# Tile tokens interleaved by four over the 32x32 blocks, one rearranging store per tile, q and k loaded per tile

## The chip, the cores and the metric

The kernel runs on one core of a Trainium2 chip. The metric is the device time of one execution in microseconds (us). Three runs of the kernel before took 1748.88 to 1751.74 us, with a median of 1751.24 us.

## What is computed

Three layers run one after the other on 8 batches of 576 tokens with a model width of 512, all in float32.

```python
# attention inside chunks of 64 tokens, 8 heads of 64
scores = scale * (q_c @ k_c.T); attn = softmax(scores); x = attn @ v_c     # (B, S, 512)
# first layer: layer norm, then a feed-forward of width 2048, with a residual
xn = (x - mean(x)) / sqrt(var(x) + 1e-6) * g_ln
x = x + relu(xn @ w_ch1) @ w_ch2
# second layer: low-rank mixing over the sequence, then another feed-forward
u = x + (x.T @ U @ V).T
out = u + relu(u @ w2_ch1) @ w2_ch2
```

The weights and U, V come as 8-byte floats; the kernel turns each weight into a high and a low float32 part and multiplies in three passes (high by high, high by low, low by high).

## The kernel before, in words

The 4608 tokens are 36 tiles of 128 tokens, three tiles to a block, so 12 blocks (0 to 11). A tile holds two chunks of 64. One program order is written out by hand in steps: in step `g` TensorE does the first product of one (block, f) pair (`g1`, 12 matmuls into the bank `psh`) and the second product of the pair two steps earlier (`g2`, 9 matmuls into `acc`). A block takes 16 steps. Between them the plan puts the attention and the normalisation of the tiles of the next block, and the turning of the second layer's weights (`pre_*`). Each engine runs its share of this one order, and waits where an operand is not there.

For blocks 3 to 11 (27 tiles) a tile passes these stages, in steps counted from a tile's start `s`. With `g` the first step of the block before its own, `s` is `g-3`, `g+1`, `g+5` for the three tiles from block 6 on, a little later for blocks 3 to 5:

- `load_qk` (SP queue, line 335): q and k of one block, features on the partitions, in pieces of 32 floats (128 bytes).
- `st_A` (VectorE, lines 379 and 380): two 32x32-block transposes, into `qt` and `kt_pl`.
- `st_Bd` (TensorE, tile `psm<-kt_pl,qt`, one step after `st_A` for the first tile of a block): scores, then maximum, subtraction and exponential (ScalarE, line 487).
- `st_Cd`: `spread` stores the exponentials in a DRAM scratch `sp` (ScalarE's queue, line 604), so that `gather` (line 609) can load the tile with its 32-blocks exchanged.
- `st_T` (VectorE, line 503): a transpose of what was gathered. `st_D`: the product with v (TensorE, `psm<-v_pl,kt_pl`; v comes by `load_v`, line 362).
- `st_N`, `st_S`, `st_E`: the normalised tile `xn` makes the same trip, `spread`, `gather`, and a transpose on VectorE (line 614), then the split in high and low parts (ScalarE line 616, GpSimd line 617). They are the right-hand side of `g1` of the tile's block.

A 32x32 transpose turns blocks in place on the partitions, so `spread` and `gather` exchange the blocks between partitions. Before, token `t` of a tile has block `a = t // 32` and place `j = t % 32`; a store that takes `a` off the partitions needs a DMA of its own for each of the four `a`.

Two more things of the program matter. The ReLU of `g1` (ScalarE line 677, high part, then VectorE line 678, low part) must be done before `g1` uses the same bank again, two steps later; it stands in order on ScalarE and VectorE behind what the plan puts there, the DMA issues of ScalarE's queue among them. And every DMA takes the next of eight completion semaphores in program order, whichever queue issues it; a DMA waits until the one eight places before it has landed. `load_qk` for a whole block waits until `st_A` of the last tile of the block before has read the tile `q6` or `k6`. The raw weight words (tile `raw`, lines 179 and 182) are loaded on SP's queue too, and are read first by ScalarE (`pre_a`, line 190).

Of the kernel before, what the change touches and what calls it, by code (L numbers as in the profile page):

```python
# [8 lines left out]
F32 = mybir.dt.float32  # L9
# [9 lines left out]
def fused_kernel(ctx, tc, q, k, v, g_ln, w1_a, w2_a, U, V, w1_b, w2_b, out):  # L19
    nc = tc.nc  # L20
# [4 lines left out]
    P = 128  # L25
    CH = 64
    NCB = S // CH
    NT = B * S // P
    TPB = 3
    BT = TPB * P  # L30
    NB = NT // TPB
    NF = DFF // P
    SB = (7, 7, 8, 7, 7)
    PRE_G, PRE_N = 168, (11, 22)
    PRE_GAPS = (4, 1, 1, 1, 1, 1, 4, 1)
    PRE_SKIP, PRE_CAP = (15, 0), {"POOL": 1}
    NPR = NF // 2
    KT = DM // P
# [10 lines left out]
    qkp = ctx.enter_context(tc.tile_pool(name="qkp", bufs=1))  # L49
# [15 lines left out]
    def f32(a):  # L65
        return a.bitcast(F32)
# [244 lines left out]
    def chunk_runs(c0, n):  # L311
        done = 0
        while done < n:
            b, s = divmod(c0 + done, NCB)
            m = min(n - done, NCB - s)
            yield done, m, b, s * CH
            done += m

    qk = {}

    def load_qk(j, part, parts_):
        todo = []
        for nm in ("q6", "k6"):
            if nm not in qk:
                qk[nm] = qkp.tile([P, 4, 4 * TPB, 32], F32, tag=nm, name=nm)
        for off, n, b, s0 in chunk_runs(2 * TPB * j, 2 * TPB):
            for nm, src in (("q6", q), ("k6", k)):
                for g in range(4):
                    for pr in range(4):
                        todo.append((  # L330
                            qk[nm][32 * g:32 * g + 32, pr, 2 * off:2 * (off + n), :],
                            src[b, 2 * pr + g // 2, s0:s0 + n * CH, (g % 2) * 32:(g % 2) * 32 + 32].rearrange("(a j) i -> j a i", j=32),
                        ))
        for o, i_ in todo[part * len(todo) // parts_:(part + 1) * len(todo) // parts_]:
            nc.sync.dma_start(out=o, in_=i_)  # L335

    E0 = 2 * TPB
    pl = {}
# [33 lines left out]
    def st_A(i):  # L376
        j, t = divmod(i, TPB)
        qt = t1.tile([P, 4, P], F32, tag="qt", name="qt")
        nc.vector.transpose(out=qt.rearrange("p h (a j) -> p h a j", a=4), in_=qk["q6"][:, :, 4 * t:4 * t + 4, :])
        nc.vector.transpose(out=pl["k"][:, 0].rearrange("p h (a j) -> p h a j", a=4), in_=qk["k6"][:, :, 4 * t:4 * t + 4, :])  # L380
        state["qt", i] = qt


# [106 lines left out]
    def st_Cd(i):  # L490
        e = state.pop(("e", i))
        spread(2 * NT + i, e)
        s2 = st.tile([P, 2, 2, 4], F32, tag="s2", name="s2")
        nc.vector.tensor_reduce(out=s2.rearrange("p h k r -> p (h k r)"), in_=e.rearrange("p (g i) -> p g i", i=32), axis=AX.X, op=ALU.add)
        sm = st.tile([P, H, 1], F32, tag="sm", name="sm")
        nc.vector.scalar_tensor_tensor(out=sm.rearrange("p (r h) o -> p h (r o)", h=2), in0=s2[:, :, 0, :], scalar=1e-9, in1=s2[:, :, 1, :], op0=ALU.add, op1=ALU.add)
        nc.vector.reciprocal(out=sm, in_=sm)
        state["s", i] = sm

    def st_T(i):  # L500
        w = state.pop(("w", 2 * NT + i))
        pt = pl["k"][:, 1]
        nc.vector.transpose(out=pt.rearrange("p r (a j) -> p a r j", a=4), in_=w.rearrange("p a (r i) -> p a r i", r=4))
        state["p", i] = (pt, state.pop(("s", i)))

    xt = {}
# [62 lines left out]
    def tiles_of(j):  # L569
        return [j * TPB + t for t in range(TPB)]  # L570

    def xt_tile(j, t):
        if t == 0:
            n = KT * P * len(tiles_of(j))
            o = (2 * n + 3 * BT) * (j % 2)
            xt[j] = tuple(act[:, o + m * n:o + (m + 1) * n].rearrange("p (k c) -> p k c", k=KT) for m in range(2))
        return (a[:, :, t * P:(t + 1) * P] for a in xt[j])
# [22 lines left out]

    def spread(key, src):
        d = dr.tile([4, 32, 4, P], F32, tag=f"sp{key}", name=f"sp{key}")
        for a in range(4):
            nc.scalar.dma_start(out=d[:, :, a, :].rearrange("g j c -> j g c"), in_=src[32 * a:32 * a + 32, :].rearrange("j (g c) -> j g c", g=4))
        state["sp", key] = d

    def gather(key):
# [3 lines left out]

    def split(j, t, w, tag):
        x = t1.tile([P, KT, P], F32, tag=tag, name="wT")
        nc.vector.transpose(out=x.rearrange("p k (a j) -> p a k j", a=4), in_=w.rearrange("p a (k i) -> p a k i", k=KT))
        hi, lo = xt_tile(j, t)
        nc.scalar.copy(out=hi, in_=x)  # L616
        nc.gpsimd.tensor_tensor(out=lo, in0=x, in1=f32(hi), op=ALU.subtract)  # L617

    def st_S(i):
        spread(i, state.pop(("n", i)))  # L620

    def st_E(i):
        split(i // TPB, i % TPB, state.pop(("w", i)), "xn")
# [88 lines left out]
    def stages(s):  # L712
        return (0, 1, 2, 3, 4, 6, 5) if s + 1 < len(SB) else range(7)

# [6 lines left out]
    NWR, NHR = 15, 8  # L721
    row0 = [sum(SB[:s]) * P for s in range(len(SB))]
    ncol = [SB[s] * P // 2 for s in range(len(SB))]
    made = {}
# [86 lines left out]
    def batches(s):  # L811
        c = 0
        while c < SB[s] * P:
            b, v0 = divmod(row0[s] + c, S)
            n = min(S - v0, SB[s] * P - c)
            yield b, c, v0, n
# [143 lines left out]
    def z_tile(s, t):  # L960
        if (s, t) not in zout:
            if s == len(SB) - 1 and t < 4:
                zout[s, t] = made["u", (s + 1) % 2][t][0]
# [169 lines left out]
    with tc.manual_schedule():  # L1133
# [12 lines left out]
        def at(g, fn, *a):  # L1146
            plan.setdefault(g, []).append((fn, a))
# [9 lines left out]
        for n in range(2, NB):  # L1157
            g = NF * (n - 1)
            ends = []
            for t, i in enumerate(tiles_of(n)):  # L1160
                if n == 2:
                    s = (10, 15, 24)[t]
                    at(s - 6, load_qk_nat, i)
                    at(s, st_A_pe, i)
                    at(s + 1, st_B, i)
                    at(s + 2, st_C, i)
                    at(s + 3, st_D, i)
                    at(s + 3, load_v, i + 1)
                    if t == 0:
                        at(5, kv_tiles, i)  # L1170
                        at(6, load_v, i)
                    ends += [(pos[0, NF - 1] - 1 + t, st_N, i), (pos[0, NF - 1] + t, st_E_pe, i)]
                else:
                    s = g + {3: (2, 5, 8), 4: (-1, 2, 5), 5: (-2, 1, 5)}.get(n, (-3, 1, 5))[t]
                    at(s - (1 if n < 5 or t == 0 else 2), st_A, i)
                    at(s, st_Bd, i)
                    at(s + 1, st_Cd, i)
                    at(s + 2, gather, 2 * NT + i)
                    at(s + 3, st_T, i)
                    at(s + 5, st_D, i)  # L1180
                    if i + 1 < NT:
                        at(s + 5, load_v, i + 1)
                    s += 4 if n == 3 else 6
                    at(s + (n == 3), st_N, i)
                    at(s + 1, st_S, i)
                    at(s + 2, gather, i)
                    at(s + 3, st_E, i)
            for x in sorted(ends, key=lambda x: (x[0], x[1] is st_N)):
                at(*x)
            if 2 <= n < NB - 1:  # L1190
                runs = len(list(chunk_runs(2 * TPB * (n + 1), 2 * TPB)))
                first, last = {2: (13, 16), 3: (8, 12), 4: (4, 9)}.get(n, (3, 9) if runs == 1 else (0, 9))
                parts_ = last + 1 - first
                for part in range(parts_):
                    at(g + first + part, load_qk, n + 1, part, parts_)
        for n in range(NB):
            g = pos[n, NF - 1] + 1
            at(g + LAG + 2, store, n)
            g = max(g, pos[1, NF - 1] + 1)
            both = any((n * TPB + t) % 9 == 4 for t in range(TPB))  # L1200
            early_z = []
            for t in range(TPB):
                i = n * TPB + t
                r = i % 9
# [59 lines left out]
        x = PRE_G  # L1264
# [88 lines left out]
        for g in range(len(seq) + LAG):  # L1353
# [19 lines left out]
            j, f = seq[g - LAG] if LAG <= g < len(seq) + LAG else (0, 0)  # L1373
# [42 lines left out]
```

## Time and profile before

| | |
|---|---|
| median of three runs | 1751.24 us (1748.88 to 1751.74) |
| the profiled execution | 1754.48 us, its span 1752.7 us |
| TensorE busy | 1660.1 us, 95% of the span |
| VectorE, ScalarE, GpSimd busy | 1186.0, 599.2, 300.3 us |
| mean granted clock of TensorE | 0.977 |
| DMA packets under 512 bytes | 197857 of 388847 |

The span is from the first to the last instruction. A busy share says how long an engine had work in hand, not that it was at its peak: at half the granted clock a matmul takes longer and counts as busy. DMA issues are not counted as busy, though an engine's later instructions wait behind them.

### The profile page before, as it was taken

What the parts mean: (1) busy time and instruction counts of PE and PEld (TensorE: products, weight loads), DVE (VectorE), ACT (ScalarE), POOL (GpSimd) and SP (SyncE); (2) the same over time, 40 slices, a digit from 0 to 9 for tenths busy, and PEclk for the clock granted to TensorE, in tenths of its full rate; (3) what the DMA queues carried; (4) which work ended last, traced back from release to release, by engine and by line L of the source; (5) the groups of instructions that cost most, each with busy time, mean ns of one, the idle gap of its engine ahead of it and who ended that gap; (6) DMA issues with size and microseconds to landing.
All of it is one profiled execution on the core that took longest, in us unless ns stands there. A gap on an engine that the chain in (4) does not pass through costs nothing.

```text
span 1752.7 us, 28378 instructions
## 1 busy us (share of the span) xinstructions
PE 1660.1 (95%) x9890; PEld 1448.8 (83%) x9890; DVE 1186.0 (68%) x2456; ACT 599.2 (34%) x1098; POOL 300.3 (17%) x291
## 2 busy tenths in 40 slices
PE   7899998998989899999999899998999999899998
PEld 5788887787878787878888798987988788798997
DVE  7888644476767676677773349737946873885686
ACT  5555311232223232223331234523443352344332
POOL 1000001111011111112021033052014204302311
PEclk8899999999999999999999999999999999999999
DMA  6443423546555664748454387778778867877874
GB/s 169 115 139 113 98 66 81 144 123 179 152 138 157 162 164 127 209 121 233 143 158 131 116 252 235 215 207 255 230 206 234 258 193 215 263 212 210 253 215 138
DMA packets 388847, 307.95 MB, mean 176 GB/s; under 512 B 197857, under 2 KB 284897, under 8 KB 388706
## 3 DMA queue, kind: packets, MB, share of 16 engines
q1 hardware_dynamic: 322818, 247.01, 50.5%
q10 hardware_dynamic: 65888, 59.14, 11.2%
q8 instruction: 79, 1.29, 0.3%
q14 instruction: 62, 0.51, 0.1%
HBM read 241.53 MB, written 64.49 MB: 175 GB/s over the span
## 4 chain that ended last, share of the span: by engine, by line
PE 52%; DMA 9%; DVE 7%; SPq 3%; issue 2%; ACT 1%; ACTq 1%; POOL 0%; DVEq 0%; POOLq 0%
PE ps L63 37%; PE acc L63 7%; PE psh L63 7%; DMA q<-in_q 2%; SPq L335 2%; DMA raw<-in_moe_w_ch 1%; DMA w<-sp 1%; DMA k<-in_k 1%; DMA zr<-zd 1%; DMA v_pl<-in_v 1%; DMA out<-zt 1%; DMA sp<-xn 1%; PE psm L63 1%; DVE act L678 1%; DMA wr<-wd 0%
## 5 line engine op out<-in xcount | busy, mean ns | idle before, releaser
L63 PE MATMUL ps<-act,wr 128*128 128x448 f32 (+1 forms) x2100 | 458.1, 375 | 9.3 <-DVE h L927 3.6
L63 PEld LDWEIGHTS ps<-act,wr 128*128 128x128 f32 x2100 | 395.0, 190 | 58.5 <-DVE h L927 4.9
L63 PE MATMUL psh<-act,w0h 128*128 128x384 f32 x1536 | 401.1, 342 | 18.6 <-DVE act L678 11.8
L63 PE MATMUL acc<-w1h,act 128*128 128x512 f32 x1152 | 404.9, 406 | 0.0
L63 PEld LDWEIGHTS psh<-act,w0h 128*128 128x128 f32 x1536 | 285.7, 191 | 40.9 <-DVE act L678 15.8
L63 PEld LDWEIGHTS acc<-w1h,act 128*128 128x128 f32 x1152 | 220.2, 191 | 57.9 <-issue 9.4
L678 DVE SCALAR_TENSOR_TENSOR act<-psh,act 128x384 fp32r<-128x384 f32 x192 | 106.7, 556 | 233.2 <-ACT act L677 232.6
L63 PE MATMUL psh<-act,w0l 128*128 128x384 f32 x768 | 262.4, 342 | 0.9 <-DVE w0l L151 0.9
L63 PE MATMUL acc<-w1l,act 128*128 128x512 f32 x576 | 230.7, 400 | 0.0
L677 ACT ACTIVATE act<-psh 128x384 fp32r<-128x384 f32 x192 | 93.7, 489 | 341.7 <-PE psh L63 231.0
L63 PEld LDWEIGHTS psh<-act,w0l 128*128 128x128 f32 x768 | 147.0, 191 | 1.2 <-DVE w0l L151 1.2
L63 PEld LDWEIGHTS acc<-w1l,act 128*128 128x128 f32 x576 | 110.3, 192 | 18.0
L617 POOL TENSOR_TENSOR act<-wT,act 128x512 fp32r<-128x512 f32 x27 | 34.8, 1290 | 317.8 <-ACT act L616 312.4
L917 ACT ACTIVATE h<-h 128x448 f32<-128x448 f32 (+1 forms) x80 | 46.2, 588 | 120.2 <-DVE h L927 92.4
L542 POOL TENSOR_SCALAR rs<-mv 128x1 f32<-128x1 f32 x36 | 10.6, 293 | 409.3 <-DVE mv L540 401.0
L923 DVE TENSOR_TENSOR h<-ps,h 128x448 f32<-128x448 f32 (+1 forms) x40 | 24.7, 632 | 75.6 <-PE ps L63 75.6
L190 ACT ACTIVATE raw<-raw 128x512 f32<-128x512 f32 x64 | 42.0, 670 | 83.6 <-DMA raw<-in_moe_w_ch 38.4
L653 POOL TENSOR_TENSOR zr<-zr 128x512 f32<-128x512 f32 x24 | 31.4, 1308 | 159.7 <-DMA zr<-zd 143.5
L910 POOL TENSOR_TENSOR h<-h,h 128x448 f32<-128x448 f32 (+1 forms) x40 | 50.5, 1274 | 47.7 <-DVE hr0l L897 24.5
L562 POOL TENSOR_TENSOR xn<-xn,gbc 128x512 f32<-128x512 f32 x27 | 38.5, 1424 | 66.1 <-DVE xn L561 66.1
L63 PE MATMUL ps<-hr0h,wr 128*128 128x448 f32 (+1 forms) x140 | 47.1, 376 | 0.3 <-issue 0.2
L63 PE MATMUL ps<-hr5h,wr 128*128 128x448 f32 (+1 forms) x140 | 46.5, 371 | 0.0
(220 smaller groups left out, 2536.9 us busy)
## 6 DMA issues: line engine op xcount, KB each, us to landing
wr<-wd SPq DMA_DIRECT2D x560, 256.0 KB
raw<-in_moe_w_ch SPq DMA_DIRECT2D x48, 512.0 KB
w<-sp ACTq DMA_DIRECT2D x54, 256.0 KB
wd<-wsp ACTq DMA_DIRECT2D x38, 256.0 KB
x1d<-x SPq DMA_DIRECT2D x36, 256.0 KB
xw<-x1d SPq DMA_DIRECT2D x144, 64.0 KB
v_pl<-in_v SPq DMA_DIRECT2D x132, 64.0 KB
raw<-in_moe_w_ch SPq DMA_DIRECT2D x64, 128.0 KB
```

What stands on the lines that cost most here:

```text
L63: nc.tensor.matmul(o, lhsT=l, rhs=r, start=start, stop=stop, **kw)
L190: nc.scalar.activation(out=w.bitcast(F32), in_=w.bitcast((F32, U32)[n]), func=AF.Copy, scale=2.0 ** (-112, -52)[n])
L335: nc.sync.dma_start(out=o, in_=i_)
L542: nc.gpsimd.tensor_scalar(out=rs, in0=mv[:, 1:2], scalar1=1e-6, scalar2=None, op0=ALU.add)
L562: nc.gpsimd.tensor_tensor(out=xn, in0=xn, in1=gbc, op=ALU.mult)
L617: nc.gpsimd.tensor_tensor(out=lo, in0=x, in1=f32(hi), op=ALU.subtract)
L653: nc.gpsimd.tensor_tensor(out=zr[:, 0], in0=zr[:, 0], in1=zr[:, 1], op=ALU.add)
L677: nc.scalar.activation(out=hi, in_=ps, func=AF.Relu)
L678: nc.vector.scalar_tensor_tensor(out=lo, in0=ps, scalar=0.0, in1=f32(hi), op0=ALU.max, op1=ALU.subtract)
L910: nc.gpsimd.tensor_tensor(out=b11, in0=b12, in1=b11, op=ALU.subtract)
L917: relu = lambda a: nc.scalar.activation(out=a, in_=a, func=AF.Relu)
L923: vt(out=c12, in0=ps, in1=c12, op=ALU.add)
```

## The change

Token `t` of a tile is now block `a = t % 4`, place `j = t // 4`. The tokens of a tile are in the same order outside; only which tokens make up a 32-block is new. Partition `p` of a tile and the row `(j, a)` of the scratch are then one and the same, so `spread` is one DMA of 128 partitions. The four transposes of a tile write tokens `4 j + a`, so neighbours in a block go to every fourth float (16 bytes) of the output, where they were next to each other before. `load_qk` works on one tile at a time: for each of q and k and each of four partition groups one DMA takes all four heads of one parity (8 DMAs a tile, 16 where a tile spans two batches), with its own steps in a table `QK_AT`.

```diff
+    QK_AT = {3: ((-3, -1), (0, 2), (3, 5)), 4: ((-11, -6), (-5, -2), (-2, 1)), 5: ((-12, -9), (-8, -5), (-4, -1)), 0: ((-13, -9), (-9, -5), (-5, -1))}
...
-    def load_qk(j, part, parts_):
+    def load_qk(i, part, parts_):
         todo = []
-        for nm in ("q6", "k6"):
-            if nm not in qk:
-                qk[nm] = qkp.tile([P, 4, 4 * TPB, 32], F32, tag=nm, name=nm)
-        for off, n, b, s0 in chunk_runs(2 * TPB * j, 2 * TPB):
+        for off, n, b, s0 in chunk_runs(2 * i, 2):
             for nm, src in (("q6", q), ("k6", k)):
+                if nm not in qk:
+                    qk[nm] = qkp.tile([P, TPB, 4, 4, 32], F32, tag=nm, name=nm)
                 for g in range(4):
-                    for pr in range(4):
-                        todo.append((
-                            qk[nm][32 * g:32 * g + 32, pr, 2 * off:2 * (off + n), :],
-                            src[b, 2 * pr + g // 2, s0:s0 + n * CH, (g % 2) * 32:(g % 2) * 32 + 32].rearrange("(a j) i -> j a i", j=32),
-                        ))
+                    r0 = 32 * g + CH // 4 * off
+                    todo.append((
+                        qk[nm][r0:r0 + CH // 4 * n, i % TPB],
+                        src[b, g // 2::2, s0:s0 + n * CH, (g % 2) * 32:(g % 2) * 32 + 32].rearrange("r (j a) i -> j a r i", a=4),
+                    ))
...
-        nc.vector.transpose(out=qt.rearrange("p h (a j) -> p h a j", a=4), in_=qk["q6"][:, :, 4 * t:4 * t + 4, :])
-        nc.vector.transpose(out=pl["k"][:, 0].rearrange("p h (a j) -> p h a j", a=4), in_=qk["k6"][:, :, 4 * t:4 * t + 4, :])
+        nc.vector.transpose(out=qt.rearrange("p r (j a) -> p a r j", a=4), in_=qk["q6"][:, t])
+        nc.vector.transpose(out=pl["k"][:, 0].rearrange("p r (j a) -> p a r j", a=4), in_=qk["k6"][:, t])
...
-        nc.vector.transpose(out=pt.rearrange("p r (a j) -> p a r j", a=4), in_=w.rearrange("p a (r i) -> p a r i", r=4))
+        nc.vector.transpose(out=pt.rearrange("p r (j a) -> p a r j", a=4), in_=w.rearrange("p a (r i) -> p a r i", r=4))
...
-        for a in range(4):
-            nc.scalar.dma_start(out=d[:, :, a, :].rearrange("g j c -> j g c"), in_=src[32 * a:32 * a + 32, :].rearrange("j (g c) -> j g c", g=4))
+        nc.scalar.dma_start(out=d.rearrange("g j a c -> (j a) g c"), in_=src.rearrange("p (g c) -> p g c", g=4))
...
-        nc.vector.transpose(out=x.rearrange("p k (a j) -> p a k j", a=4), in_=w.rearrange("p a (k i) -> p a k i", k=KT))
+        nc.vector.transpose(out=x.rearrange("p k (j a) -> p a k j", a=4), in_=w.rearrange("p a (k i) -> p a k i", k=KT))
...
-            if 2 <= n < NB - 1:
-                runs = len(list(chunk_runs(2 * TPB * (n + 1), 2 * TPB)))
-                first, last = {2: (13, 16), 3: (8, 12), 4: (4, 9)}.get(n, (3, 9) if runs == 1 else (0, 9))
+
+        for n in range(3, NB):
+            for t, i in enumerate(tiles_of(n)):
+                first, last = QK_AT[n][t] if n in QK_AT else QK_AT[0][t]
                 parts_ = last + 1 - first
                 for part in range(parts_):
-                    at(g + first + part, load_qk, n + 1, part, parts_)
+                    at(NF * (n - 1) + first + part, load_qk, i, part, parts_)
```

The order of the matmuls on TensorE, of the work on GpSimd and of everything but the stores and loads named is as it was; line numbers shift by up to five. On ScalarE's queue each `spread` is one row. Here is one place, the store of a normalised tile (`sp<-xn`) with its neighbours, before:

```order
L253 DMA wd_2_134<-wsp 128x512
L677 ACTIVATE act<-psh 128x384
L604 DMA sp_4459<-xn 32x4x128 x4
L677 ACTIVATE act<-psh 128x384
L609 DMA w<-sp_4459 128x512
```

And now:

```order
L254 DMA wd_2_134<-wsp 128x512
L672 ACTIVATE act<-psh 128x384
L599 DMA sp_4345<-xn 128x4x128
L672 ACTIVATE act<-psh 128x384
L604 DMA w<-sp_4345 128x512
```

Four issues stood between two evacuations of `psh`; one stands there now, at the same place.

On SP's queue the loads of q and k move. Before, around the raw weight loads of the block that runs at 480 to 512 us of the profile (the loads are those of block 7):

```order
L335 DMA q_2209<-in_q 32x6x32 x4
L335 DMA k_2210<-in_k 32x6x32 x3
L179 DMA raw<-in_moe_w_ch 128x1024
L335 DMA k_2210<-in_k 32x6x32 x13
L179 DMA raw<-in_moe_w_ch 128x1024
L362 DMA v_pl<-in_v 64x4x64 x4
L179 DMA raw<-in_moe_w_ch 128x1024 x2
```

And the same raw loads now:

```order
L335 DMA k_2210<-in_k 32x16x32 x2
L335 DMA q_2209<-in_q 16x16x32 x3
L180 DMA raw<-in_moe_w_ch 128x1024
L335 DMA q_2209<-in_q 16x16x32
L335 DMA k_2210<-in_k 16x16x32 x4
L335 DMA q_2209<-in_q 16x16x32
L180 DMA raw<-in_moe_w_ch 128x1024
L358 DMA v_pl<-in_v 64x4x64 x4
L335 DMA q_2209<-in_q 16x16x32 x3
L335 DMA k_2210<-in_k 16x16x32 x4
L335 DMA q_2209<-in_q 32x16x32 x4
L335 DMA k_2210<-in_k 32x16x32 x2
```

Thirteen loads between two raw loads became six, and loads of the later tiles now stand behind the second raw load, where there were none.

## Rows read from the trace of the kernel before

**Rows 1.** Busy time in two stretches: us, each engine's busy (instructions), clock, DMA share, GB/s

```profile
210.00:930.00 720.00, 686.25 (x4862) 591.35 (x4861) 473.47 (x994) 191.20 (x364) 101.93 (x110) 0.98 0.55 147
1000.00:1752.00 752.00, 723.77 (x3421) 640.74 (x3420) 518.36 (x1051) 289.24 (x521) 179.20 (x147) 0.99 0.75 223
```

**Rows 2.** Waits of TensorE, 210 to 930 us: total, times, longest

```profile
PE psm L63 <- DVE kt_pl L380: 14.6, 8, 3.0
PE psh L63 <- DVE act L678: 10.1, 5, 2.8
PE psm L63 <- DMA v_pl<-in_v: 4.2, 2, 2.4
```

**Rows 3.** Last and sum of seven stretches of low clock, 210 to 930 us

```profile
917.70:921.10 3.40, 3.40 (x12) 3.02 (x11) 0.56 (x1) 0.49 (x1) 0.00 (x0) 0.50 0.45 150
sum 30.60, PE 27.28 PEld 22.74 DVE 22.81 ACT 7.48 POOL 3.26; mean PE 3.90 PEld 3.25 DVE 3.26 ACT 1.07 POOL 0.47
```

**Rows 4.** Waits of ScalarE, 210 to 930 us

```profile
ACT act L677 <- DMA sp<-xn: 40.8, 9, 9.3
ACT raw L190 <- DMA raw<-in_moe_w_ch: 38.4, 10, 6.5
ACT act L677 <- DMA sp<-e: 19.4, 5, 5.1
ACT act L677 <- DMA k<-in_k: 10.3, 3, 7.5
```

**Rows 5.** Waits of SP's own queue, whole span

```profile
SPq L335 <- DMA sp<-xn: 23.9, 13, 4.9
SPq L362 <- DMA sp<-xn: 14.1, 3, 6.6
```

**Rows 6.** ScalarE in order of time, 266 to 287 us: start, us, what, idle before

```profile
282.21 1.79 ACTq L604 DMA_DIRECT2D sp<-xn  x4
284.10 0.49 ACT L677 ACTIVATE act<-psh 128x384 fp32r<-128x384 f32 x1 [7.04 <-DMA sp<-xn]
```

**Rows 7.** ScalarE in order of time, 498 to 518 us

```profile
510.27 0.65 ACT L190 ACTIVATE raw<-raw 128x512 f32<-128x512 f32 x1 [3.56 <-DMA raw<-in_moe_w_ch]
```

**Rows 8.** SP's queue in order of time, 494 to 516 us

```profile
497.97 8.46 SPq L335 DMA_DIRECT2D k<-in_k  x13
506.54 0.38 SPq L179 DMA_DIRECT2D raw<-in_moe_w_ch  x1
```

**Rows 9.** VectorE in order of time, 504 to 518 us

```profile
511.33 0.56 DVE L678 SCALAR_TENSOR_TENSOR act<-psh,act 128x384 fp32r<-128x384 f32 x1 [1.98 <-ACT act L677]
...
516.43 0.67 DVE L380 STREAM_TRANSPOSE kt_pl<-k 128x512 f32<-128x512 f32 x1
```

**Rows 10.** TensorE in order of time, 510 to 518 us

```profile
511.95 0.62 PE L63 MATMUL psh<-act,w0h 128*128 128x384 f32 x2 [1.74 <-DVE act L678]
...
517.25 0.69 PE L63 MATMUL psm<-kt_pl,qt 64*64 64x64 f32 x32 [2.94 <-DVE kt_pl L380]
```

**Rows 11.** TensorE in order of time, 359 to 364.5 us

```profile
363.77 0.69 PE L63 MATMUL psm<-kt_pl,qt 64*64 64x64 f32 x32 [0.25 <-DVE kt_pl L380]
```

**Rows 12.** VectorE's transposes by line and form: busy us, mean ns, idle before

```profile
L379 DVE STREAM_TRANSPOSE qt<-q 128x512 f32<-128x512 f32 x27 | 18.9, 700 | 0.0
L380 DVE STREAM_TRANSPOSE kt_pl<-k 128x512 f32<-128x512 f32 x27 | 18.1, 671 | 0.4 <-DMA x1d<-x 0.4
...
L973 DVE STREAM_TRANSPOSE zt<-rs 128x128 f32<-128x128 f32 x23 | 8.9, 388 | 6.3 <-POOL rs L956 6.3
...
L973 DVE STREAM_TRANSPOSE zt<-ux 128x64 f32<-128x64 f32 x14 | 2.1, 259 | 2.7 <-DMA out<-zt 2.7
```

**Rows 13.** Issues that write the scratch sp: ns least/median/most, first and last start

```profile
L604 ACTq DMA_DIRECT2D sp<-e x108: 309/450/2108, 224.0 to 878.5; - x108
L604 ACTq DMA_DIRECT2D sp<-xn x108: 309/444/2013, 249.3 to 902.3; - x108
```

**Rows 14.** Issues of line 335 on SP's queue

```profile
L335 SPq DMA_DIRECT2D q<-in_q x192: 311/441/1516, 196.6 to 808.3; - x192
L335 SPq DMA_DIRECT2D k<-in_k x192: 311/461/2344, 204.9 to 821.3; - x192
```

## The prediction

> **What bounds the kernel now.** I read first the busy time by stretch, then who waited for whom on TensorE, then the same two engines in order of time around the longest waits. TensorE is the bound: in the stretch from 210 to 930 us, in which the changed instructions lie, it is busy 686.25 of 720 us, and VectorE 473.47 [rows 1]. The stretch after 1000 us, 752 us long, holds none of them. So the change can act only on the 34 us in which TensorE is idle there, and on what those stalls cost in clock.
>
> Three waits make up most of these 34 us: 14.6 us for the transposed k of `st_A` (8 times, all of them the first tile of a block), 10.1 us for the low half of the ReLU, which frees the bank `psh` (5 times), and 4.2 us for v (twice) [rows 2]. [...]
>
> **Why TensorE waits.** ScalarE has lots of idle time, but it stands in order. Its ReLU waited 40.8 and 19.4 us behind the stores `sp<-xn` and `sp<-e` and 10.3 us for loads of k, and its first reading of raw weights waited 38.4 us for their DMA [rows 4]. The ReLU needs nothing of k: it stood behind a store whose completion semaphore was still held by an earlier load. At 282.21 us four stores are issued after a wait, and the ReLU at 284.10 us comes after 7.04 us of idle ScalarE [rows 6]. The other way round, SP's loads of q and k waited 23.9 us, and those of v 14.1 us, for `sp<-xn` to land [rows 5], which holds no data of theirs. The queues hold each other up through the round of eight semaphores. The second form is on SP alone: thirteen k loads take 8.46 us from 497.97 us on, the raw load behind them is issued at 506.54 us [rows 8], ScalarE reads it at 510.27 us after 3.56 us idle [rows 7], so VectorE's half of the ReLU comes late at 511.33 us and the transposed k is ready only at 517.1 us [rows 9]; TensorE stalls 1.74 us and then 2.94 us [rows 10].
>
> **The change part by part.**
>
> *Stores.* 27 tiles with two trips, four issues each, are 216 [rows 13]; now there are 54. At a median of 0.45 us ScalarE's queue saves 162 x 0.45 = 73 us of issuing at most. The new issue is four old ones in one: between 0.31 us (the least of the rows) and 4 x 0.45 = 1.8 us (nothing saved); I take 0.5 us, since old issues of very different size have nearly the same median (0.45 for 64 KB here, 0.44 for the 24 and 48 KB loads of q [rows 14]). None of it is on TensorE's path by itself: it is TensorE's wait for `psh` and for k that shows it.
>
> *Loads.* 384 issues [rows 14] become 27 x 8 plus 8 for each of three tiles that span two batches: 240. Bytes and 128-byte pieces stay the same. They are spread over all 16 steps, where they were bunched in 7 (10 where a block spans two batches).
>
> *The round of eight.* In 16 steps a usual block issued 32 loads of q and k, 12 of v, 24 stores and 6 gathers, 74 besides the weights; now 24 + 12 + 6 + 6 = 48. Blocks that span two batches go from 106 to 56. Eight semaphores thus reach back over 1.5 to 1.9 times as much time, and I expect most waits of [rows 4, 5] that come from q, k and `sp` to go. Of the 10.1 us for the ReLU I take four of five away: -8 us, with bounds of 0 and -10.1. The loads of v stand on SP's queue among those of q and k and wait for the same round [rows 5]; in the order now, two to four loads stand between them where 11 to 16 stood: -4 us, with bounds 0 and -4.2.
>
> *Transposes.* Four a tile now write every fourth float. No row has such a write of 512 columns. The nearest is the output transpose of the second layer, which writes at the same step: 388 ns for 128 columns, 259 ns for 64 [rows 12], so 129 ns for 64 more and, as an estimate, 388 + 6 x 129 = 1162 ns for 512, against 700 and 671 ns now [rows 12]. The bounds are no change, and 4 x 388 = 1552 ns. I take 1162: 0.95 us more for q and k together, about 0.48 us each for the other two, 27 x 1.9 = 51 us of VectorE's time. VectorE goes from 473 to 525 of 720 us and has room on average. But `st_A` of a block's first tile has one step of lead only, and there it lands on the path. Where ScalarE had not been late (block 5, at 363.77 us) TensorE waited just 0.25 us for k [rows 11]; that becomes 0.25 + 0.95 = 1.2 us. If all nine first tiles come to this, the k wait goes from 14.6 to 11 us: -4 us. Bounds: all gone, -14.6; or each of the eight present waits grows by 0.95 and by one more transpose in VectorE's queue, 0.48: +11.4. The later tiles of blocks 3 and 4 also have their scores one step behind `st_A`; I add one such 0.95 for them: +1 us. The other two transposes of a tile have a step or more behind them; what hides them is also that three issues, 3 x 0.45 = 1.35 us, go ahead of the gather. Without that cover they would cost the start of a block 0.5 us each.
>
> [...]
>
> *Clock.* With the waits for `psh` and v gone, the stretches of low clock that follow them have less cause, while k waits of some 1.2 us remain. I take less than half of the 13.6 us: -6 us, with bounds 0 and -13.6.
>
> **The sum.** -8 - 4 - 4 + 1 - 6 = -21 us. The profiled execution took 1754.48 us (1.8 us more than its span); it lies 3.2 us over the median of the runs, so I set the sum against the median: 1751.24 - 21 = 1730 us. The likeliest case's own range is 1718 to 1743 us.
>
> **Rivals.**
>
> 1. *The strided transposes win* (slower). In the last steps of a block VectorE has the wT transpose, two steps of weight work and `st_A` in a row. If the raw loads stay late, the waits for `psh` stay, k waits grow by 11.4 us from a mean of 14.6 / 8 = 1.8 us to 3.2 us each, and these bring low clock to some five more blocks at 1.7 us (half of the 3.4 us of [rows 3]), +8.5: 1771 us. For it: 108 transposes, 51 us, on the engine that TensorE waits for most. Against: VectorE was idle for 1.98 us just before the worst case, waiting for ScalarE [rows 9]. It decides once k waits grow by more than 17 / 8 = 2.1 us in a block, since 8 + 4 + 6 - 1 = 17 us are to be gained elsewhere; with half of that gained, 1771 - 8 = 1763 us.
> 2. *The raw loads stay late* (about no change). Loads of q and k now stand between all raw loads of a block. If these still come 3 to 4 us late, the 38.4 us remain, only v and a little clock are gained, and the transposes eat it: 1744 to 1755, say 1750 us. The same follows if one store of 128 partitions holds the queue as long as four did, which would mean that the change does not do what it says. Against: six issues stand where thirteen stood.
> [...]
> 4. *The step of 16 bytes costs these transposes nothing*: no 0.95 us on any of nine first tiles, 1730 - 8.6 = 1721 us. The row of 388 ns speaks against it, since a quarter of 700 is 175. [...]
>
> **How the numbers follow.** A measurement of this kernel tells about 0.2% (3.5 us) from no change. Likeliest case 0.52, rival 1 0.18, rival 2 0.15, rival 3 0.08, rival 4 0.07. The range runs from 1710 to 1758 us: some 0.04 lies below, 0.14 above. Faster: 0.52 + 0.08 + 0.07 and a third of rival 2, 0.72; the same 0.09; slower 0.19.
>
> **What would show it.** Right: `spread` with 54 issues near 0.5 us; ScalarE's waits for `sp` and k far below 70 us together, those for raw below 20; TensorE's waits for the ReLU under 4 us and for v at zero; the four transposes near 1.16 us; k waits about 1 us each. Wrong: transposes near 0.7 or over 1.5 us; k waits over 3 us at every block start; ScalarE's waits for raw as large as before; a stretch after 1000 us that is not as long as now.

## The result, and the profile after

The changed kernel takes 1723.97 us (median of 4 runs, 1720.94 to 1729.75) against 1751.49 us for the kernel before on the same chip (4 runs, 1748.88 to 1758.9): a ratio of 0.984, 95% interval 0.9801 to 0.988. Its profiled execution took 1723.31 us, span 1721.5 us.

Busy time of the changed kernel in the stretch of the layers' overlap, columns as in [rows 1]:

```profile
210.00:930.00 720.00, 705.48 (x5011) 610.13 (x5010) 520.08 (x1029) 197.18 (x373) 107.10 (x112) 1.00 0.55 153
```

TensorE is busy for 705 of 720 us, where it was 686, though VectorE has 47 us more to do (part of which is that the faster kernel gets further in the same stretch). The answer to [rows 2], TensorE's waits there (total, times, longest):

```profile
PE psm L64 <- DVE kt_pl L376: 9.4, 6, 3.0
PE psh L64 <- ACT act L611: 1.8, 2, 1.6
PE psh L64 <- POOL act L612: 1.8, 2, 0.9
PE psh L64 <- DVE x L690: 1.6, 1, 1.6
```

The waits for the ReLU (10.1 us) and for v (4.2 us) are gone; those for k are 5.2 us shorter. Two stretches of the lower clock, 0.50, are left where [rows 3] had seven:

```profile
580.40:583.80 3.40, 3.40 (x10) 2.79 (x9) 3.30 (x9) 0.98 (x2) 0.00 (x0) 0.50 0.39 105
887.60:891.00 3.40, 3.40 (x11) 3.40 (x12) 0.00 (x0) 0.00 (x0) 0.00 (x0) 0.50 0.70 216
sum 6.80, PE 6.80 PEld 6.19 DVE 3.30 ACT 0.98 POOL 0.00; mean PE 3.40 PEld 3.10 DVE 1.65 ACT 0.49 POOL 0.00
```

ScalarE's waits, the answer to [rows 4]:

```profile
ACT act L672 <- PE psh L64: 214.0, 88, 5.6
...
ACT raw L191 <- DMA raw<-in_moe_w_ch: 17.1, 8, 4.6
...
ACT act L672 <- DMA sp<-xn: 4.5, 2, 2.8
```

The ReLU (L672) now waits for TensorE's own result, as it should; behind the stores it stands for 4.5 us instead of 60.2, and the raw weights are late by 17.1 us instead of 38.4. The price is in the transposes [rows 12], by line and form (busy us, mean ns, idle before):

```profile
L499 DVE STREAM_TRANSPOSE kt_pl<-w 128x512 f32<-128x512 f32 x27 | 29.7, 1101 | 16.8 <-DMA w<-sp 16.8
L375 DVE STREAM_TRANSPOSE qt<-q 128x512 f32<-128x512 f32 x27 | 29.6, 1097 | 0.0
L609 DVE STREAM_TRANSPOSE wT<-w 128x512 f32<-128x512 f32 x27 | 29.6, 1096 | 6.3 <-DMA q<-in_q 3.8 <-issue 2.4 <-DMA w<-sp 0.2
L376 DVE STREAM_TRANSPOSE kt_pl<-k 128x512 f32<-128x512 f32 x27 | 29.3, 1083 | 0.0
```

And the issues of the stores and loads, which answer to [rows 13, 14] (ns least/median/most):

```profile
L599 ACTq DMA_DIRECT2D sp<-e x27: 366/377/1801, 225.6 to 846.3; - x27
L599 ACTq DMA_DIRECT2D sp<-xn x27: 366/377/637, 250.9 to 870.1; - x27
```

```profile
L335 SPq DMA_DIRECT2D q<-in_q x120: 578/617/1109, 198.1 to 800.3; - x120
L335 SPq DMA_DIRECT2D k<-in_k x120: 578/628/2838, 201.1 to 812.7; - x120
```

Where the time went: between 210 and 930 us the three waits give 28.9 - 9.4 = 19.5 us. At a clock of 0.50 the next matmul starts 0.320 us after one into `psh` and 0.427 us after one into `acc`, against 0.174 and 0.231 us at 1.00 (medians between 210 and 930 us, the same in both traces). So 46% of TensorE's time in these stretches is put down to the clock, an estimate from those starts: 0.46 x 27.28 = 12.5 us before [rows 3] and 0.46 x 6.80 = 3.1 us now, 9.4 us less. Together that is 28.9 us, of a span that is 31.2 us shorter. The last ReLU of the first layer starts at 967.6 us where it started at 994.9 us, so 27.3 us come from before that point. Up to there TensorE does the same 6446 matmuls, first in the kernel before, then in the changed one:

```profile
0.00:994.88 994.88, 931.26 (x6446) 803.57 (x6447) 663.69 (x1398) 307.45 (x572) 121.10 (x144) 0.97 0.52 141
0.00:967.60 967.60, 918.27 (x6446) 795.46 (x6447) 697.62 (x1398) 308.57 (x572) 123.65 (x144) 0.98 0.53 145
```

Its idle time falls by 14.3 us (63.6 to 49.3) and its busy time by 13.0 us. That is less idle time than the three waits give, mostly because in the first 210 us TensorE is idle for 29.1 us where it was 25.3. The remaining 3.9 us lie in work that holds none of the changed instructions, and single runs of either kernel differ by that much.

### The profile page after: what moved, and what is told of

Same layout as the page of the kernel before. It is cut to its first block, busy times and chain, and to the rows that moved or that the text cites. A ratio compares the mean times of both kernels' runs of the same rounds, so it can differ in the third digit from the quotient of the medians.

```text
span 1721.5 us, 27974 instructions
## 1 busy us (share of the span) xinstructions
PE 1644.8 (96%) x9890; PEld 1439.9 (84%) x9890; DVE 1218.9 (71%) x2456; ACT 599.9 (35%) x1098; POOL 302.7 (18%) x291
## 4 chain that ended last, share of the span: by engine, by line
PE 59%; DMA 6%; DVE 6%; issue 1%; POOL 1%; ACT 1%; SPq 1%; ACTq 0%; DVEq 0%; POOLq 0%
PE ps L64 32%; PE acc L64 13%; PE psh L64 12%; DMA zr<-zd 3%; PE psm L64 1%; DMA out<-zt 1%; DMA wr<-wd 1%; DMA raw<-in_moe_w_ch 1%; PE zps L64 1%; DMA xw<-x1d 1%; DMA w<-sp 0%; POOL zr L648 0%; DVE zt L968 0%; PE pslow L64 0%; SPq L979 0%
## 5 line engine op out<-in xcount | busy, mean ns | idle before, releaser
L64 PE MATMUL psh<-act,w0h 128*128 128x384 f32 x1536 | 399.6, 341 | 10.7 <-DVE act L673 3.3
L672 ACT ACTIVATE act<-psh 128x384 fp32r<-128x384 f32 x192 | 93.8, 489 | 341.9 <-PE psh L64 278.3
L191 ACT ACTIVATE raw<-raw 128x512 f32<-128x512 f32 x64 | 42.6, 674 | 53.3 <-DMA raw<-in_moe_w_ch 17.1
```

What stands on the lines that cost most here:

```text
L64: nc.tensor.matmul(o, lhsT=l, rhs=r, start=start, stop=stop, **kw)
L191: nc.scalar.activation(out=w.bitcast(F32), in_=w.bitcast((F32, U32)[n]), func=AF.Copy, scale=2.0 ** (-112, -52)[n])
L672: nc.scalar.activation(out=hi, in_=ps, func=AF.Relu)
```

## The experiments

Three theories stood at the start. Mine was that both halves of the change count, by the number of DMAs. The rivals: only the loads count (A), only the store counts (B). The kernels were timed on several chips, on which the kernel before has medians of 1751.5 to 1754.9 us; the tables therefore give, beside the median, the ratio to the kernel before on the same chip, and it is the ratios that compare. They also give from each kernel's one profiled execution, 210 to 930 us: TensorE's waits for k, for the ReLU's second half and for v; ScalarE's ReLU behind stores (`sp`), and ScalarE's first step on raw weights behind their DMA (raw). All in us; 0 stands where the profile lists no such wait.

**The parts one by one.**

| kernel | median | ratio, 95% interval | k | ReLU | v | sp | raw |
|---|---|---|---|---|---|---|---|
| before | 1751.5 | 1 | 14.6 | 10.1 | 4.2 | 60.2 | 38.4 |
| changed | 1724.0 | 0.984 (0.9801 to 0.988) | 9.4 | 0 | 0 | 4.5 | 17.1 |
| store alone | 1743.8 | 0.994 (0.992 to 0.9959) | 18.7 | 5.0 | 2.1 | 5.0 | 45.2 |
| loads alone | 1723.7 | 0.9835 (0.9809 to 0.9862) | 9.9 | 1.1 | 0 | 53.7 | 8.1 |
| changed, store cut in four | 1735.9 | 0.9901 (0.9873 to 0.9928) | 15.0 | 1.6 | 0 | 54.2 | 14.1 |
| changed, contiguous transposes | 1714.3 | 0.9775 (0.9748 to 0.9802) | 3.7 | 0 | 0 | 5.1 | 9.7 |

*Store alone*: the kernel before with

```
-        for a in range(4):
-            nc.scalar.dma_start(out=d[:, :, a, :].rearrange("g j c -> j g c"), in_=src[32 * a:32 * a + 32, :].rearrange("j (g c) -> j g c", g=4))
+        nc.scalar.dma_start(out=d.rearrange("g j a c -> (j a) g c"), in_=src.rearrange("p (g c) -> p g c", g=4))
...
-        nc.vector.transpose(out=pt.rearrange("p r (a j) -> p a r j", a=4), ...
+        nc.vector.transpose(out=pt.rearrange("p r (j a) -> p a r j", a=4), ...
```

and the same in `split`.

> The kernel before with the new rearranging store alone (one DMA for a tile, and the strided transposes behind the gathers); q and k are loaded by block as before. My theory (fewer issues on ScalarE's queue and fewer turns in the eight completion semaphores shared by all hardware queues, so the ReLUs and v's conversion come in time; the k load is untouched): the ReLU waits (10.1 us before) fall to under 4 us, the k waits stay at about 15 us, some low-clock stretches go; 1736 to 1744 us against 1751.5. Rival A (the gain is that of the loads): 1749 us or more, ReLU waits as before.

1743.8 us, near the upper end of my band: the store alone is worth 0.6%. The ReLU waits fell to 5.0 us, not under 4. The row that matters is the one that did not move. ScalarE in the store-alone kernel:

```profile
ACT raw L190 <- DMA raw<-in_moe_w_ch: 45.2, 14, 6.8
...
ACT act L676 <- DMA sp<-xn: 5.0, 2, 2.9
```

Its ReLUs no longer stand behind stores, and the raw weights are as late as ever. TensorE still waits for ReLUs, and waits 4 us more for k. (The profiled execution took 1751.32 us, the longest of the 12, so its waits are rather too large for the median.)

*Loads alone*: the changed kernel with the two edits above undone.

> The changed kernel with the old store (four DMAs for a tile, contiguous transposes behind the gathers); q and k are loaded per tile and spread over the steps, and their transposes are strided. My theory (both parts take DMAs out of the same shared turn of semaphores, the loads a part of the k waits): 1733 to 1743 us, ReLU waits between 2 and 8 us, k waits as in the changed kernel, 8 to 12 us. Rival A (all of the gain is that of the loads and where they are issued): 1722 to 1728 us. Rival B (all of it is the store's): 1748 us or more.

1723.7 us: rival A, and my theory missed. ScalarE in the loads-alone kernel:

```profile
ACT act L673 <- DMA sp<-e: 28.1, 7, 5.4
ACT act L673 <- DMA sp<-xn: 25.6, 7, 8.5
...
ACT raw L191 <- DMA raw<-in_moe_w_ch: 8.1, 6, 3.4
```

And TensorE's wait for the ReLU in it:

```profile
PE psh L64 <- DVE act L674: 1.1, 1, 1.1
```

The ReLUs stand behind the four stores nearly as long as before, up to 8.5 us at a time, and TensorE waits 1.1 us for them in all. So once the loads are spread, the waits behind the stores are long but hardly on the path. While raw weights are late they do count: the store alone halves the ReLU waits (10.1 to 5.0 us) with raw weights no earlier.

*Store cut in four*: the changed kernel with

```
-        nc.scalar.dma_start(out=d.rearrange("g j a c -> (j a) g c"), in_=src.rearrange("p (g c) -> p g c", g=4))
+        for g in range(4):
+            nc.scalar.dma_start(out=d[g].rearrange("j a c -> (j a) c"), in_=src[:, g * P:(g + 1) * P])
```

> The changed kernel with its rearranging store cut by its index g into four DMAs of all 128 partitions, 64 KB each: the same bytes in the same pieces of 512 bytes, tokens interleaved as in the changed kernel, but four issues and four semaphores again. My theory (the number of issues is what counts): the store's part of the gain is given back, 1732 to 1742 us, and some ReLU waits come back. Rival (a store of 128 partitions instead of 32 lands sooner, so the gathers come sooner; the number does not matter): 1722 to 1728 us, no ReLU waits.

1735.9 us, as my theory has it for the number of issues, and with four issues the waits for `sp` are back at 54.2 us; but the loss is in the waits for k (15.0 us), and the ReLU waits hardly came back (1.6 us).

*Contiguous transposes*: the changed kernel with `(j a)` turned into `(a j)` in its four transposes.

> The changed kernel with its four kinds of VectorE transposes written contiguously, so that the tokens of each tile stay in the interleaved order (the token order is left out, everything else runs the same). It prices the 16-byte step of the transposes' output: 4 transposes for each of 27 tiles, each 0.39 us shorter by the two traces. My theory: most of VectorE's time is off the path; the k waits fall from 9.4 us by some 0.8 us for each first tile of a block, to 4 to 6 us, and the whole to 1716 to 1721 us. Rival C (the longer transposes delay VectorE's ReLUs and much else, and took half of the change's gain): 1705 to 1713 us. Rival D (they are hidden altogether): 1723 to 1725 us.

1714.3 us, between my band and rival C's; by ratio 0.65% under the changed kernel. Taken by its ratio to the chip of the result it is 0.9775 x 1751.5 = 1712 us, inside rival C's band. The k waits fell to 3.7 us and no stretch of low clock is left between 210 and 930 us.

**What it is in the loads: their number, or their place.** The change makes 240 issues of 384 and spreads them. Theory 2, formed on the runs above: raw weights are on SP's queue too, and stand behind a bunch of loads.

| kernel | median | ratio, 95% interval | k | ReLU | v | raw |
|---|---|---|---|---|---|---|
| bunched, steps -13 to -7 | 1755.2 | 1.0018 (1.0003 to 1.0033) | 20.1 | 6.5 | 2.1 | 48.2 |
| steps -13 to -4 | 1732.5 | 0.9889 (0.9864 to 0.9914) | 13.4 | 1.5 | 0 | 35.3 |
| changed, steps -13 to -1 | 1724.0 | 0.984 (0.9801 to 0.988) | 9.4 | 0 | 0 | 17.1 |
| loads in halves, 480 issues | 1798.2 | 1.0256 (1.0235 to 1.0276) | 44.4 | 13.1 | 0 | 69.1 |
| before, steps -13 to -4 | 1755.9 | 1.0009 (0.9982 to 1.0035) | 21.3 | 1.8 | 2.3 | 13.6 |

*Bunched*: only the table of steps differs.

```
-    QK_AT = {3: ((-3, -1), (0, 2), (3, 5)), 4: ((-11, -6), (-5, -2), (-2, 1)), 5: ((-12, -9), (-8, -5), (-4, -1)), 0: ((-13, -9), (-9, -5), (-5, -1))}
+    QK_AT = {3: ((-3, -2), (-2, -1), (-1, 0)), 4: ((-8, -7), (-7, -5), (-5, -4)), 5: ((-12, -11), (-11, -9), (-9, -7)), 0: ((-13, -11), (-11, -9), (-9, -7))}
```

> The changed kernel with its loads of q and k issued in fewer steps: from the fifth block on in steps -13 to -7 before the block (six steps for the three tiles) where the changed kernel has -13 to -1, and in two to five steps for the two blocks before; 240 issues as in the changed kernel. The first runs showed that the loads alone give the whole gain. Theory 2 (it is the spread: raw weights, v and the completion semaphores no longer stand behind a bunch of q and k loads on SP's queue): 1735 to 1745 us, ScalarE's waits for raw weights back at 30 us or more and the ReLU waits at 4 us or more. Rival E (it is the number of issues, 240 against 384): 1722 to 1728 us.

1755.2 us: the whole gain is gone, which is more than theory 2 had expected. That the strided transposes, which stay, make up the difference is likely, but a bunched kernel with contiguous ones was not run. One block shows how. SP's queue in the bunched kernel, in order of time (start, us, what):

```profile
724.30 7.66 SPq L335 DMA_DIRECT2D k<-in_k  x3
732.00 1.27 SPq L335 DMA_DIRECT2D q<-in_q  x2
733.37 0.55 SPq L636 DMA_DIRECT2D zd<-z  x1
733.96 1.26 SPq L335 DMA_DIRECT2D q<-in_q  x2
735.26 4.25 SPq L335 DMA_DIRECT2D k<-in_k  x4
739.56 1.29 SPq L335 DMA_DIRECT2D q<-in_q  x2
740.95 0.59 SPq L183 DMA_DIRECT2D raw<-in_moe_w_ch  x1
```

ScalarE and then TensorE in the same kernel:

```profile
746.12 0.66 ACT L191 ACTIVATE raw<-raw 128x512 f32<-128x512 f32 x1 [11.29 <-DMA raw<-in_moe_w_ch]
...
747.21 0.47 ACT L672 ACTIVATE act<-psh 128x384 fp32r<-128x384 f32 x1
```

```profile
748.33 0.62 PE L64 MATMUL psh<-act,w0h 128*128 128x384 f32 x2 [3.18 <-DVE act L673]
...
759.85 1.13 PE L64 MATMUL psm<-kt_pl,qt 64*64 64x64 f32 x32 [3.41 <-DVE kt_pl L376]
```

Thirteen loads keep the raw load back from 724.30 to 740.95 us. Not all of that is issuing: 13 issues at the median of 0.63 us are 8 us, and in the same stretch the loads themselves wait 7.6 us for DMAs of the other queue that hold none of their data:

```profile
SPq L335 <- DMA w<-sp: 5.8, 2, 4.1
SPq L335 <- DMA wd<-wsp: 1.8, 1, 1.8
```

So what stands before the raw load brings its own waits in the shared semaphores with it, 7.6 us here. ScalarE stands 11.29 us for it, with the next ReLU in line; TensorE loses 3.18 us for that ReLU, and 3.41 us for k, whose transposes VectorE reaches late. It is the picture of [rows 7 to 10], with an 11 us wait for 3.6 us.

Loads by tile also end another wait of SP's queue, the one for the tile of a whole block to be read. First in the kernel before, then in the bunched one:

```profile
SPq L335 <- DVE qt L379: 18.7, 6, 9.9
SPq L335 <- DVE qt L375: 0.5, 1, 0.5
```

It is gone in the bunched kernel too, and the gain is not there, so this is not what carries it by itself.

*Steps -13 to -4*: the rows of `QK_AT` for block 5 and from block 6 on end at -4 instead of -1.

> The changed kernel with its loads from the fifth block on issued over about nine steps before the block (-13 to -4), between the bunched run (six steps, 1755 us) and the changed kernel (twelve, 1724 us). Theory 2: between the two, 1732 to 1745 us, and ScalarE's waits for raw weights between 17 and 48 us. If one place alone does the harm (the steps -13 to -7): near 1755 or near 1724 us.

Between the two, as theory 2 expected, in time (1732.5 us) and in the wait for raw weights (35.3 us).

*Halves*: each load split over its partitions, in the same steps.

```
-                    r0 = 32 * g + CH // 4 * off
...
+                    for m in range(2):
+                        r0 = 32 * g + CH // 4 * off + CH // 8 * n * m
+                        s1 = s0 + n * CH // 2 * m
```

> The changed kernel with each load of q and k cut in two by partitions (16 and 16; 8 and 8 where a tile spans two batches): 480 issues instead of 240, so more than the 384 of before, in the same steps and with the same pieces. Theory 2 (the spread counts): 1723 to 1730 us. Rival E (the number of issues counts): 1738 us or more, with ScalarE's waits for raw weights and the ReLU waits back.

1798.2 us: the number of issues, or the queue time that goes with it, counts as well, and theory 2 alone is refuted. Issues of the half loads:

```profile
L337 SPq DMA_DIRECT2D q<-in_q x240: 578/612/1857, 197.5 to 882.9; - x120
L337 SPq DMA_DIRECT2D k<-in_k x240: 578/612/2361, 203.1 to 894.7; - x120
```

A load of half the bytes occupies the queue about as long as a whole one (0.612 us against 0.617 for q and 0.628 for k), so by the medians 480 of them take 294 us of it against 149 us (240 at about 0.62 us), and 173 us before (384 at 0.45 us). SP's waits for a DMA at the load line, all added up, rise too, from 99.6 us to 180.6 us; this run does not tell the longer issuing from these waits.

*Before, steps -13 to -4*: can the old loads by block be spread?

```
-                first, last = {2: (13, 16), 3: (8, 12), 4: (4, 9)}.get(n, (3, 9) if runs == 1 else (0, 9))
+                first, last = {2: (13, 16), 3: (8, 12), 4: (4, 9)}.get(n, (3, 12) if runs == 1 else (0, 12))
```

> The kernel before with its loads of q and k issued over the steps -13 to -4 before a block (ten steps, where it has seven), which is as far as its buffer by block allows; 384 issues, nothing else changed. Theory 2 (what counts is how many loads stand between two loads of raw weights): a part of the gain without any interleaving, 1738 to 1747 us, ScalarE's waits for raw weights under 30 us. If the gain needs the small number of issues as well: 1748 to 1755 us.

No gain. In the profiled execution the spread did its work on raw weights (13.6 us) and on the ReLU (1.8 us), and made k itself late, so early raw weights alone do not give the gain. VectorE in this kernel, a wait that the kernel before does not have:

```profile
DVE kt_pl L380 <- DMA k<-in_k: 18.9, 4, 6.3
```

The first tile's transposes run in step -4 here, just as the last loads are issued. (The profiled execution took 1740.44 us, the shortest of the 12; the median is 1755.86 us.) What the loads by tile give is room: the third tile's loads may come after the first tile's transposes. Whether 384 loads by tile, spread as in the changed kernel, would gain as much was not run, so the smaller number is not shown to be needed.

**The transposes of the first tile, and both parts together.**

| kernel | median | ratio, 95% interval | k | ReLU | v | sp | raw |
|---|---|---|---|---|---|---|---|
| changed, first tile earlier | 1712.1 | 0.9775 (0.9759 to 0.9792) | 2.3 | 0 | 0 | 4.6 | 15.4 |
| loads alone, first tile earlier | 1720.3 | 0.9827 (0.9804 to 0.985) | 4.7 | 0.7 | 0 | 67.9 | 10.7 |
| before, first tile earlier | 1739.1 | 0.9936 (0.9914 to 0.9957) | 3.1 | 10.2 | 4.2 | 62.2 | 37.8 |
| changed, contiguous behind the gathers | 1719.9 | 0.982 (0.9803 to 0.9837) | 7.1 | 0 | 0 | 5.5 | 15.2 |

*First tile earlier*, the same line in all three kernels:

```
-                    at(s - (1 if n < 5 or t == 0 else 2), st_A, i)
+                    at(s - (1 if n < 5 else 2), st_A, i)
```

> The changed kernel with the transposes of q and k of each block's first tile one step earlier from the sixth block on, as those of the second and third tile already are. Seven of the nine first tiles concern it, where TensorE waits for k in the changed kernel. If those waits and the low clock behind them are what is left: k waits from 9.4 to under 4 us and 1715 to 1720 us, as good as contiguous transposes gave. If the moved transposes only delay VectorE's other work (ReLU, raw weights) at that place: 1722 to 1728 us, with ReLU waits of 3 us or more.

> The loads-alone kernel (store in four, contiguous transposes behind the gathers) with the first tile's transposes of q and k one step earlier from the sixth block on. If the store matters no more once the loads are spread and k is early: 1709 to 1715 us, the same as the changed kernel with that step (1712 us). If the one store is what keeps the rest in time there: 1718 us or more.

> The kernel before with the transposes of q and k of each block's first tile one step earlier from the sixth block on. The k waits are 14.6 us there and that step took 12 us from the changed kernel. If the k waits of before were only the missing step of lead: 1737 to 1743 us. If they were VectorE's and ScalarE's lateness behind raw weights, which the step leaves as it is: 1745 to 1752 us.

The changed kernel with it takes 1712.1 us, below the band: the fastest here that leaves nothing out, 2.25% under the kernel before. TensorE's waits in it:

```profile
PE psh L64 <- POOL act L612: 3.0, 4, 0.9
PE psm L64 <- DVE kt_pl L376: 2.3, 2, 1.7
```

The kernel before gains 0.64% by the same line. Its waits with it, TensorE's first, then ScalarE's for raw weights:

```profile
PE psh L63 <- DVE act L678: 10.2, 7, 3.1
PE psm L63 <- DVE kt_pl L380: 3.1, 1, 3.1
ACT raw L190 <- DMA raw<-in_moe_w_ch: 37.8, 10, 6.1
```

The k waits go though raw weights are as late as ever: they were the missing step of lead, while the waits for ReLU and v stay untouched. With the loads alone it came out at 1720.3 us, outside what I expected if the store mattered no more, and the two intervals do not meet: once the transposes have their lead, the one store, with the strided writes behind the gathers that belong to it, is worth about 0.5% (0.9827 - 0.9775) after all. On which wait was not followed.

*Contiguous behind the gathers*: `st_T` and `split` of the changed kernel with `(a j)`.

> The changed kernel with the two transposes behind the gathers written contiguously (st_T and split; those of q and k keep the strided write); the token order of the tiles behind the gathers is left out. With the changed kernel, the kernel with the loads alone and the store in four it makes a square: one or four issues, strided or contiguous behind the gathers (1724, 1724, 1736 us). If one issue and contiguous writes add up: 1724 + 1724 - 1736 = 1712 us. If both only took the same wait away, so that either is enough: 1720 to 1725 us. The kernel with all four contiguous took 1714 us.

1719.9 us; the ratio is 0.002 under the changed kernel's, and the two intervals overlap. So one store and contiguous writes do not add up: with the store in four the strided writes cost 0.66% (0.9901 against 0.9835), with one store 0.2% or nothing. That square is not quite clean, since the four stores of its two corners are cut differently (by columns and by partitions).

## Why the prediction was right, and where its steps were not

The forecast was 1730 us, the result 1724 us, in the likeliest case and its range. The bound, the waits and the price of the transposes were right; the path by which the change was to end the waits was only half right, so that the ReLU term came out near its size is in part luck. Step by step:

- **The bound** held: what is gained is TensorE's waits in that stretch and their clock.
- **ReLU, -8 us**: -10.1 us. **v, -4 us**: -4.2 us. Both right in size, not in their reasons. The ReLU term was put down to the waits for q, k and `sp`; with the loads alone those for `sp` stay and all but 1.1 us of it is gained. For v I counted two to four loads between those of v; from 440 us on 4 to 15 loads of q and k stand between one group of v loads and the next, where up to 26 stood.
- **k, -4 and +1 us**: -5.2 us in all. The first tiles' waits that remain average 9.4 / 6 = 1.6 us, near the 1.2 us reckoned, and the transposes, estimated at 1162 ns, take 1083 to 1101 ns.
- **Clock, -6 us**: about -9.4 us. This is the mis-sized term: I took less than half of 13.6 us, which was an estimate of mine, half of the 27.28 us of [rows 3]. No run shows that half; the matmuls' starts give 46%, 12.5 us, and three quarters of it went. Each of the seven stretches begins within 4.1 us of the start of an idle time of TensorE of 0.9 to 3.0 us. With 2.1 us more on the ReLU, 0.2 us more on v and 2.2 us more on k the terms come to 28.9 us, 7.9 more than the 21 reckoned. The medians differ by only 27.5 us; the 3.8 us of more idle time in the first 210 us, which no term held, go the other way.
- **Store issues**: 0.377 us, where I took 0.5 us.
- **"The round of eight" is the step that failed.** In the trace of the kernel before all 1951 DMAs, 1577 on SP's queue and 374 on ScalarE's, take eight semaphores in turn, 243 or 244 each, and 1821 of them wait for the one they take directly before they are issued; in the changed kernel there are 1645, 205 or 206 each. I expected fewer DMAs to reach further back in the shared semaphores and so to end the waits for q, k and `sp`. SP's waits for a DMA at the load line, all added up, did not fall: 86.2 us before, 99.6 us after, 89.6 us in the bunched kernel. ScalarE's waits for `sp` did fall, but because of its own stores: one store ends them (5.0 us), loads alone do not (53.7 us). And with the loads spread they are little of TensorE's loss: with 53.7 us of them left the time is the same. I had built the ReLU term on [rows 6], a 7 us wait, without asking whether TensorE stood still there. What carried the gain is where the loads stand, the second form that I described, on SP [rows 7 to 10]: the same 240 issues, bunched, make raw weights late by 48.2 us and gain nothing. The waits for raw weights do not set the time by themselves, though: the store alone gains 0.6% with 45.2 us of them, and the old loads, spread, gain nothing with 13.6 us.
- **"They are spread over all 16 steps"** stood in the prediction as a side remark with no term of its own, and it is 13 steps of 16 by the table (-13 to -1). The bunched run shows that without the spread nothing is gained. That more issues, with the queue time they bring, undo it is shown by the halves; that fewer than before are needed is not.
- **The strided transposes**: rival 4 (a free step of 16 bytes) is refuted by the rows of 1.08 to 1.10 us against 0.70 and 0.67 us. Rival 1 (they win) did not happen, but it had its place right: contiguous ones give 0.65%, and a step of lead for the first tile gives as much.
- **Rival 2** (raw loads stay late) is what the bunched kernel does: 48.2 us of waits for raw weights and 1755 us, against 1750 us worked out there.

Still open: why the strided writes behind the gathers cost 0.66% with the store in four and 0.2% or nothing with one. The k waits show where (15.0 against 9.9 us), not which of VectorE's operations came late.

## What to carry to other kernels

A long wait on an engine that stands in order has no price until the bound engine is seen waiting behind it: with the loads spread, 54 us of ScalarE's waits behind stores left TensorE waiting 1.1 us. Two causes of one wait do not add up: the store alone gave 0.6%, the loads alone 1.65%, both together 1.6%. Where several streams share one issuing queue, first look at what stands between two loads of the stream that is on the path, and give buffers a grain (a tile, not a block) that lets the others be spread. When an edit makes an operation longer, look for the one place where it has a single step of lead, and move it there before counting its cost.

## What the runs showed of the hardware

- How long an issue occupies its queue did not go by its bytes: by the medians 0.377 us for one store of 256 KB, where stores of 64 KB, four in a row, took 0.443 to 0.450 us each (0.31 us at the least, against 0.366 us for the large one); 0.617 us for the q and 0.628 us for the k loads of 64 and 32 KB that run over four indices, 0.612 us for their halves, against 0.441 and 0.461 us for the older ones of 48 and 24 KB over three.
- VectorE's 128x512 transposes, written at a step of 16 bytes, took 1.08 to 1.10 us, about 0.4 us more than the contiguous ones of the kernel before (0.67 to 0.71 us), whether the tokens came from a load or from a gather.
